# Two key blocks of a sliding-window attention merged into one 128 x 128 square before the transposition

## The chip, the cores and the metric

The kernel runs on one core of one Trainium2 chip. The metric is the time of one execution on the device in microseconds. A core has five engines with a queue of instructions each: TensorE (PE in the profile, with its weight loads apart as PEld), VectorE (DVE), ScalarE (ACT), GpSimd (POOL) and SyncE (SP), which issues most transfers. An engine takes its instructions in the order in which they stand in its queue, and an instruction waits at the head of the queue until the semaphores that it names have come.

## The reference

Attention with a window of 128 keys and 4 sink keys for 4 batches of 8 heads, 768 positions and a head dimension of 64, and then a feed-forward layer with a squared ReLU:

```python
scores = (1 / np.sqrt(D)) * np.matmul(q, k.transpose(0, 1, 3, 2))
is_sink = pos[None, :] < n_sink                  # 4
rel = pos[:, None] - pos[None, :]
keep = is_sink | ((rel >= 0) & (rel < window))   # 128
scores = np.where(keep, scores, -1e9)
a = np.exp(scores - scores.max(-1, keepdims=True))
a = a / (a.sum(-1, keepdims=True) + 1e-9)
x = np.matmul(a, v)                  # then heads side by side: 3072 x 512
h = x @ w_in                         # 512 -> 2048
g = s * np.maximum(h, 0) ** 2 + b
out = g @ w_out                      # 2048 -> 512
```

With a window of 128, a block of 128 queries sees only two blocks of keys besides the sinks: its own (the key's place at or below the query's) and the one before (the key's place above the query's). In a square of 128 x 128 the two parts are disjoint and fill it.

## The kernel before

Everything is fp32 at the ends. The matmuls take numbers split into a high and a low part of a shorter format (tiles `kh` and `kl`, `hl[:, 0]` and `hl[:, 1]`), so that products come as three or two matmuls on the parts.

The 3072 rows are handled in eight chunks of 384 (a half sequence, `half` 0 or 1, of one batch). The feed-forward layer of a chunk (`moe_steps`: 16 groups `l1` of 12 matmuls into `h`, 16 groups `l2` of 9 matmuls into three accumulators `po`) runs while the attention of the next chunk is made; the code calls a step of the one and a slot of the other in turn. The first two chunks' attention comes from `plain_slots`, beside the loading and splitting of the weights; it isn't touched, except for the constants. The other six, four of them second halves, come from `attn_slots`.

There the work is in units (h, i): head h, block i of three blocks of queries. `unit_a` makes the scores `sc` of a unit in PSUM (L297, L298: own block, the block before and 8 sink columns, 264 wide; 136 for the first block of a sequence), then on DVE the masked minimum of the negated scores (L302, with the mask from `msk`; its result is the row's maximum, `negm`), then the exponential on ACT (L308) into `sm`, and a copy of the sink columns on POOL (L310). `unit_b`, two slots later, transposes the two blocks of `sm` (L321, L322) into a PSUM tile `tp`, copies them on ACT into the high part of `hl` (L326) and subtracts on DVE for the low part (L327). `unit_c`, four slots after `unit_a`, multiplies `hl` with the values `vv` into `o` (L360); for i = 1 it takes what became ready for i = 0 and 1, for i = 2 the rest. PSUM tiles `sc`, `tp`, `h`, `o` share five buffers of one pool.

What decides the order in which the instructions stand in each queue is a scheduler. It takes the program in the order of the calls, with the dependences, and by costs of its own it brings forward what can go and puts back what would have to wait. A change in one place can thus move other instructions.

Of the kernel before, what the change touches and what calls it, by code (L numbers as in the profile page):

```python
# [40 lines left out]
def tile_kernel(ctx, tc, qT, kT, k0, v, vsk, n_sink, window, w, s, b, out):  # L41
    nc = tc.nc
    w, n_sink, window = (a.bitcast(I32) for a in (w, n_sink, window))
    const = ctx.enter_context(tc.tile_pool(name="const", bufs=1))
# [87 lines left out]
    def constants2():  # L132

        for i, sel in enumerate(sels):
            spread = wk.tile([P, P], F32, tag="y", name="spread", bufs=1)
            nc.gpsimd.memset(spread, 0.0)
# [5 lines left out]
            nc.scalar.copy(sel, spread)
        for t in psks:
            nc.gpsimd.memset(t, 0.0)
# [6 lines left out]
        mask(m_1[:, 2 * P:], tm2[:, :NS])
        mask(m_even[:, P:P + NS], snk[:, :NS])
        cp = nc.gpsimd.tensor_copy
        upm, lom = m_full[2][:, P:2 * P], m_full[2][:, 2 * P:]
        cp(out=m_0[:, NS:], in_=lom)
        for m, l0 in ((m_1, P), (m_even, P + NS), (m_odd, P)):
            cp(out=m[:, :P], in_=upm)
            cp(out=m[:, l0:l0 + P], in_=lom)
# [126 lines left out]
    def unit_a(k, h, i):  # L285

        hd = k.heads[h]
        pp = k.pairs[h // 2]
# [8 lines left out]
        nc.tensor.matmul(sc[:, :n], hd.qs[:, qs], hd.kh[:, c0:c0 + n], start=True, stop=False)  # L297
        nc.tensor.matmul(sc[:, :n], hd.qs[:, qs], hd.kl[:, c0:c0 + n], start=False, stop=True)  # L298
# [3 lines left out]
        nc.vector.tensor_tensor_reduce(out=sm[:, :n], in0=sc[:, :n], in1=m, scale=-0.125, scalar=BIG,  # L302
                                       op0=ALU.add, op1=ALU.min, accum_out=negm[:, uu])
# [4 lines left out]
        nc.scalar.activation(sm[:, :n], sm[:, :n], AF.Exp, bias=negm[:, uu], scale=-1.0, accum_out=pp.zz[:, i, hh:hh + 1])  # L308
# [1 line left out]
        nc.gpsimd.tensor_copy(out=pp.psk[:, i, :96].rearrange("p (t x) -> p t x", t=3)[:, :, r0:r0 + NS],  # L310
                              in_=sm[:, s0:s0 + NS].unsqueeze(1).to_broadcast([P, 3, NS]))

    def unit_b(k, h, i):

        sm, c0, p0, _ = k.cc.pop((h, i))
# [4 lines left out]
        if p0 is not None:  # L320
            nc.tensor.transpose(tp[:, :P], sm[:, p0:p0 + P], ident)  # L321
        nc.tensor.transpose(tp[:, P:2 * P], sm[:, c0:c0 + P], ident)  # L322

        a, z = (P if p0 is None else 0), 2 * P
        hi, lo = (hd.hl[:, t, i * z + a:(i + 1) * z] for t in range(2))
        nc.scalar.copy(hi, tp[:, a:z])  # L326
        nc.vector.tensor_tensor(out=lo, in0=tp[:, a:z], in1=hi.bitcast(F32), op=ALU.subtract)  # L327
        pp = k.pairs[h // 2]
        if h % 2 == 1 and i == BLK - 1:
            zr = wk.tile([P, 2, BLK, 2], F32, tag="zr", name="zr")  # L330
            zh = wk.tile([P, BLK, 2], F32R, tag="zh", name="zh")
            nc.vector.tensor_scalar(out=zr[:, 0], in0=pp.zz, scalar1=1e-9, scalar2=None, op0=ALU.add)
# [473 lines left out]
```

## Time and profile before

| | us |
|---|---|
| median of 3 executions | 771.59 (771.5 to 771.79) |
| the profiled execution | 772.53 |
| its span, first to last instruction | 770.7 |
| PE, DVE, ACT, POOL busy | 732.8, 492.0, 471.3, 233.3 |

The span has three parts. Up to about 145 us the weights are loaded and split beside the plain attention. From there to 697 us six chunks of attention run beside the MoE of the chunk before; then comes the last chunk's MoE alone. In the profile's rows L12 is line 12 of the kernel, `out<-in` names the tiles, the numbers behind the bar are the group's busy time and the mean ns of one. An entry such as `<-PE sc L298 61.6` says that the engine stood idle for 61.6 us in front of these instructions until that one came. A matmul's duration in a row is longer than the step from one to the next, since matmuls overlap; the chain of waits shows the steps.

### The profile page before, as it was taken

Reading aid. Unit: us, or ns where it says so; the run is one execution under the profiler, and the core shown is the slowest. Engines: PE = TensorE matmul, PEld = TensorE weight load, DVE = VectorE, ACT = ScalarE, POOL = GpSimd, SP = SyncE. Lnnn points to the kernel's source line nnn. Section 1 sums busy time; section 2 is a strip of 40 time slices with the busy share of each in tenths; the row PEclk is TensorE's granted clock in tenths of the full one; section 3 lists DMA queues with packets and bytes.
Section 4 is the critical chain, followed back from the end, with each engine's and each line's share of the span. In section 5 each row is a group of like instructions: output and inputs, shape, how many; then the busy total and the mean of one; then the engine's idle time right before and its main releaser. Section 6 shows DMA issues by size and latency. Waiting matters only on the chain.

```text
span 770.7 us, 11928 instructions
## 1 busy us (share of the span) xinstructions
PE 732.8 (95%) x3988; PEld 649.2 (84%) x3988; DVE 492.0 (64%) x1210; ACT 471.3 (61%) x1176; POOL 233.3 (30%) x380
## 2 busy tenths in 40 slices
PE   7977788899999999999999999999999999999996
PEld 4665577789989899989989899899989999899885
DVE  7879989636676566765676466755676466753321
ACT  4987748537676666646676566656676576643222
POOL 4134633213243332413242242323243233301000
PEclk9999889999999999999999999999999999999999
DMA  8954032022121221112112212112112212001001
GB/s 175 379 216 162 17 125 76 11 80 67 53 53 53 69 56 57 31 50 86 33 44 66 68 46 61 36 51 70 45 45 69 68 43 67 15 1 42 0 1 46
DMA packets 32309, 52.62 MB, mean 68 GB/s; under 512 B 9841, under 2 KB 20721, under 8 KB 30321
## 3 DMA queue, kind: packets, MB, share of 16 engines
q1 hardware_dynamic: 31152, 51.59, 21.8%
q8 instruction: 34, 0.56, 0.3%
q10 hardware_dynamic: 1088, 0.20, 0.2%
q14 instruction: 35, 0.28, 0.1%
HBM read 45.49 MB, written 6.29 MB: 67 GB/s over the span
## 4 chain that ended last, share of the span: by engine, by line
PE 78%; DVE 9%; ACT 3%; issue 2%; POOL 1%; DMA 1%; ACTq 0%; DVEq 0%; POOLq 0%
PE h L575 32%; PE po L593 30%; PE o L360 5%; PE sc L298 2%; PE sc L297 2%; PE tp L322 2%; DVE w L205 2%; PE tp L321 2%; DVE r L579 1%; DVE w L218 1%; DVE wt L204 1%; DVE sm_p L503 1%; DVE g L582 1%; PE o L528 1%; PE os L385 1%
## 5 line engine op out<-in xcount | busy, mean ns | idle before, releaser
L593 PE MATMUL po<-w,g 128*128 128x512 f32 x1152 | 300.1, 403 | 5.1 <-DVE g L582 2.8
L575 PE MATMUL h<-x,w 128*128 128x384 f32 x1536 | 299.8, 344 | 3.3 <-ACT w L212 3.3
L575 PEld LDWEIGHTS h<-x,w 128*128 128x128 f32 x1536 | 268.1, 191 | 10.2 <-ACT w L212 3.7
L593 PEld LDWEIGHTS po<-w,g 128*128 128x128 f32 x1152 | 209.4, 189 | 49.0 <-DVE g L582 5.2
L578 ACT ACTIVATE r<-h 128x384 f32<-128x384 f32 x128 | 62.8, 491 | 121.4 <-PE h L575 117.5
L579 DVE SCALAR_TENSOR_TENSOR r<-r,sb 128x384 f32<-128x384 f32 x128 | 90.0, 703 | 57.9 <-ACT r L578 57.8
L582 DVE SCALAR_TENSOR_TENSOR g<-r,sb,g 128x384 fp32r<-128x384 f32 x128 | 82.6, 645 | 50.0 <-ACT g L581 48.3
L302 DVE CUSTOM_DVE_ANT_0 sm<-sc,msk 128x264 f32<-128x264 f32 (+1 forms) x144 | 59.7, 415 | 79.4 <-PE sc L298 68.6
L581 ACT ACTIVATE g<-r,sb 128x384 fp32r<-128x384 f32 x128 | 78.7, 615 | 32.1 <-DVE r L579 30.2
L310 POOL COPY psk<-sm 128x24 f32<-128x24 f32 x144 | 34.0, 236 | 190.4 <-ACT sm L308 189.5
L308 ACT ACTIVATE sm<-sm,negm 128x264 f32<-128x264 f32 (+1 forms) x144 | 72.8, 505 | 21.0 <-DVE negm L302 19.3
L277 POOL TENSOR_TENSOR kl<-kraw,kh 128x528 fp32r<-128x528 f32 (+1 forms) x48 | 60.0, 1251 | 57.6 <-ACT kh L275 53.5
L326 ACT CAST hl<-tp 128x256 fp32r<-128x256 f32 (+1 forms) x144 | 51.4, 357 | 29.0 <-PE tp L322 28.5
L327 DVE TENSOR_TENSOR hl<-tp,hl 128x256 fp32r<-128x256 f32 (+1 forms) x144 | 58.2, 404 | 10.4 <-ACT hl L326 9.5
L360 PE MATMUL o<-hl,vv 128*128 128x256 f32 (+1 forms) x352 | 61.5, 293 | 0.0
L282 POOL TENSOR_TENSOR vv<-vraw,vv 128x256 fp32r<-128x256 f32 (+1 forms) x48 | 34.5, 719 | 64.2 <-ACT vv L281 61.4
L207 POOL TENSOR_TENSOR w<-w 128x1024 int32<-128x1024 int32 (+1 forms) x17 | 33.0, 1946 | 53.4 <-DVE w L205 24.4
L360 PEld LDWEIGHTS o<-hl,vv 128*128 128x128 f32 x352 | 48.0, 190 | 0.5
L369 DVE TENSOR_TENSOR xm<-o,y 64x384 f32<-64x384 f32 x48 | 26.6, 553 | 30.0 <-ACT y L368 24.4
L298 PE MATMUL sc<-kl,qs 128*128 128x264 f32 (+1 forms) x144 | 41.0, 285 | 0.0
L297 PE MATMUL sc<-kh,qs 128*128 128x264 f32 (+1 forms) x144 | 40.0, 278 | 0.0
L322 PE MATMUL tp<-identr,sm 128*128 128x128 f32 x144 | 39.1, 272 | 0.0
(128 smaller groups left out, 867.3 us busy)
## 6 DMA issues: line engine op xcount, KB each, us to landing
w<-in_w SPq DMA_DIRECT2D x15, 1024.0 KB, 8.1
kraw<-in_kT SPq DMA_DIRECT2D x32, 264.0 KB, 2.6
out<-ot SPq DMA_DIRECT2D x24, 256.0 KB, 2.0
qraw<-in_qT SPq DMA_DIRECT2D x24, 192.0 KB, 2.4
vraw<-in_v SPq DMA_DIRECT2D x16, 256.0 KB, 2.7
kraw<-in_kT SPq DMA_DIRECT2D x16, 200.0 KB, 2.4
vsraw<-in_vsk SPq DMA_DIRECT2D x24, 64.0 KB, 1.8
vraw<-in_v SPq DMA_DIRECT2D x8, 192.0 KB, 2.3
```

What stands on the lines that cost most here:

```text
L277: nc.gpsimd.tensor_tensor(out=hd.kl[:, :kw], in0=hd.k[:, :kw], in1=hd.kh[:, :kw].bitcast(F32), op=ALU.subtract)
L298: nc.tensor.matmul(sc[:, :n], hd.qs[:, qs], hd.kl[:, c0:c0 + n], start=False, stop=True)
L302: nc.vector.tensor_tensor_reduce(out=sm[:, :n], in0=sc[:, :n], in1=m, scale=-0.125, scalar=BIG, op0=ALU.add, op1=ALU.min, accum_out=negm[: ...
L308: nc.scalar.activation(sm[:, :n], sm[:, :n], AF.Exp, bias=negm[:, uu], scale=-1.0, accum_out=pp.zz[:, i, hh:hh + 1])
L327: nc.vector.tensor_tensor(out=lo, in0=tp[:, a:z], in1=hi.bitcast(F32), op=ALU.subtract)
L360: nc.tensor.matmul(hd.o[:, q0:q0 + n * P], hd.vv[:, kb, :], hd.hl[:, t, c0 * P:(c0 + n) * P], start=(hd.n == 0), stop=(i == BLK - 1 and kb ...
L575: nc.tensor.matmul(h[:, :CH], weight[f][:, 0, wi, cc * P:(cc + 1) * P], x[xi][:, cc, :], start=(i == 0), stop=(i == 11))
L578: nc.scalar.activation(r, h[:, :CH], AF.Relu, scale=1.0 / WUP)
L579: nc.vector.scalar_tensor_tensor(out=r, in0=r, scalar=s_ap, in1=r, op0=ALU.mult, op1=ALU.mult)
L581: nc.scalar.activation(gg[:, 0, :], r, AF.Identity, bias=b_ap, scale=1.0)
L582: nc.vector.scalar_tensor_tensor(out=gg[:, 1, :], in0=r, scalar=b_ap, in1=gg[:, 0, :].bitcast(F32), op0=ALU.add, op1=ALU.subtract)
L593: nc.tensor.matmul(po[tb], gg[:, gi, tsl], weight[f][:, 1, wi, :], start=(f == 0 and i == 0), stop=(f == NF - 1 and i == 2))
```

## The change

After the scores, a predicated copy on DVE puts, inside PSUM, the part of the one block that the query can see over the part of the other block that it can't. One square of 128 columns and the 8 sink columns (136) are then masked, reduced and exponentiated in place of 264. Each unit has one transposition, and the three of a head go into one tile `tp`. After the third, the square is taken apart again: what belongs to the block before is copied on ACT (`hi_p`), what belongs to the own block is multiplied by a mask on DVE (`hi_c`), both low parts are subtracted on DVE (`lo_p`, `lo_c`), and three masks on POOL (`affine_select`) put zeros where `hi_p`, `lo_p` and `lo_c` hold the other block's numbers. The matmuls into `o` read `hl` as before.

```diff
-    msk = const.tile([P, 3 * W + P + NS], MDT, tag="msk", name="msk")
+    msk = const.tile([P, 3, P + NS], MDT, tag="msk", name="msk")
+    m_0, m_1, m_2 = (msk[:, j] for j in range(3))
+    is_cur = const.tile([P, P], U8, tag="is_cur", name="is_cur")
+    is_prev = const.tile([P, P], U8, tag="is_prev", name="is_prev")
+    cur_t = const.tile([P, P], MDT, tag="cur_t", name="cur_t")
...
-        for m, l0 in ((m_1, P), (m_even, P + NS), (m_odd, P)):
-            cp(out=m[:, :P], in_=upm)
-            cp(out=m[:, l0:l0 + P], in_=lom)
+        nc.vector.tensor_tensor(out=tmp, in0=low, in1=upp, op=ALU.add)
+        mask(m_2[:, :P], tmp)
+        nc.vector.tensor_scalar(out=is_cur, in0=rel, scalar1=0.0, scalar2=None, op0=ALU.is_ge)
+        nc.vector.tensor_scalar(out=is_prev, in0=rel, scalar1=0.0, scalar2=None, op0=ALU.is_lt)
+        nc.vector.tensor_scalar(out=cur_t, in0=rel, scalar1=0.0, scalar2=None, op0=ALU.is_le)
...
+        a = 0
+        if g % 2:
+            a = P
+            nc.vector.copy_predicated(sc[:, P:2 * P], is_prev, sc[:, :P])
+        elif g:
+            nc.vector.copy_predicated(sc[:, :P], is_cur, sc[:, P + NS:W])
+        n = P + NS
...
-        nc.vector.tensor_tensor_reduce(out=sm[:, :n], in0=sc[:, :n], in1=m, scale=-0.125, scalar=BIG,
-                                       op0=ALU.add, op1=ALU.min, accum_out=negm[:, uu])
+        nc.vector.tensor_tensor_reduce(out=sm[:, :n], in0=sc[:, a:a + n], in1=(m_0, m_1, m_2)[min(g, 2)], scale=-0.125,
+                                       scalar=BIG, op0=ALU.add, op1=ALU.min, accum_out=negm[:, uu])
...
         if i == 0:
+            hd.tp = ps("tp")
+        nc.tensor.transpose(hd.tp[:, i * P:(i + 1) * P], sm[:, c0:c0 + P], ident)
+        if i == BLK - 1:
             hd.hl = wk.tile([P, 2, 2 * CH], F32R, name="hl", tag="hl", bufs=HLB)
-        tp = ps("tp")
-        if p0 is not None:
-            nc.tensor.transpose(tp[:, :P], sm[:, p0:p0 + P], ident)
-        nc.tensor.transpose(tp[:, P:2 * P], sm[:, c0:c0 + P], ident)
...
-        nc.scalar.copy(hi, tp[:, a:z])
-        nc.vector.tensor_tensor(out=lo, in0=tp[:, a:z], in1=hi.bitcast(F32), op=ALU.subtract)
+            i0 = 1 - k.half
+            hi_p, lo_p = (hl[:, t, i0:, 0] for t in range(2))
+            hi_c, lo_c = (hl[:, t, :, 1] for t in range(2))
+            def keep(x, n, cur):
+                d = 1 if cur else -1
+                nc.gpsimd.affine_select(out=x, in_=x, pattern=[[0, n], [d, P]], fill=0.0, base=0, channel_multiplier=-d,
+                                        compare_op=ALU.is_ge if cur else ALU.is_gt)
+            nc.scalar.copy(hi_p, tp[:, i0:])
+            nc.vector.tensor_tensor(out=hi_c, in0=tp, in1=cur_t.unsqueeze(1).to_broadcast([P, BLK, P]), op=ALU.mult)
+            nc.vector.tensor_tensor(out=lo_p, in0=tp[:, i0:], in1=hi_p.bitcast(F32), op=ALU.subtract)
+            nc.vector.tensor_tensor(out=lo_c, in0=tp, in1=hi_c.bitcast(F32), op=ALU.subtract)
+            keep(hi_p, BLK - i0, False)
+            keep(lo_p, BLK - i0, False)
+            keep(lo_c, BLK, True)
```

How the queues change is seen in the order of the built programs. A row names the line, the operation, the tiles and the shape; x9 counts equal rows, and the brackets name whose semaphores the instruction waits for. The lines of the changed kernel are some numbers higher (L332 is the transposition, L386 o, L601 h, L619 po).

TensorE's queue before, for the first head of a second-half chunk, from its second unit's transpositions to its first o:

```order
L321 MATMUL tp<-identr,sm 128x128 [waits DVE_49,Activation_49]
L322 MATMUL tp<-identr,sm 128x128
L593 MATMUL po<-w_522,g 128x512 x9
L297 MATMUL sc<-kh,qs 128x264 [waits DVE_49]
L298 MATMUL sc<-kl,qs 128x264
L321 MATMUL tp<-identr,sm 128x128 [waits DVE_49,Activation_49]
L322 MATMUL tp<-identr,sm 128x128
L360 MATMUL o<-hl,vv 128x256 [waits Activation_49]
L360 MATMUL o<-hl,vv 128x256
L360 MATMUL o<-hl,vv 128x128 x2
```

The same head in the changed kernel, from its third unit's transposition:

```order
L332 MATMUL tp<-identr,sm 128x128 [waits Activation_49]
L619 MATMUL po<-w_524,g 128x512 x2
L619 MATMUL po<-w_524,g 128x512 [waits DVE_49]
L619 MATMUL po<-w_524,g 128x512 x6
L302 MATMUL sc<-kh,qs 128x264 [waits DVE_49,PE_49]
L303 MATMUL sc<-kl,qs 128x264
L332 MATMUL tp<-identr,sm 128x128 [waits PE_49,Activation_49]
L332 MATMUL tp<-identr,sm 128x128 [waits Activation_49]
L619 MATMUL po<-w_583,g 128x512 x3
L386 MATMUL o<-hl,vv 128x256 [waits Pool_49]
```

The first o now stands behind three matmuls of the next group and waits for POOL; three matmuls of an h group follow it, and then the second o, which waits for POOL again.

DVE's queue for the same head, from the predicated copy of its neighbour's scores to the low parts:

```order
L310 COPY_PREDICATED sc<-is_cur,sc 128x128 [waits PE_49]
L605 SCALAR_TENSOR_TENSOR r<-r,sb 128x384 [waits Activation_49]
L314 ISA sm,negm<-sc,msk 128x136 [waits DVE_49,Pool_49]
L314 ISA negm 128x1
L348 TENSOR_TENSOR hl<-tp,cur_t 128x3x128 [waits Activation_49]
L608 SCALAR_TENSOR_TENSOR g<-r,sb,g 128x384 [waits Activation_49]
L349 TENSOR_TENSOR hl<-tp,hl 128x3x128
L350 TENSOR_TENSOR hl<-tp,hl 128x3x128 [waits DVE_49]
```

The product (L348) waits for ACT's copy out of the same PSUM tile, and r and g of the MoE stand between the parts. POOL's queue in a head of a first-half chunk:

```order
L344 AFFINE_SELECT hl<-hl 128x2x128 [waits DVE_49]
L344 AFFINE_SELECT hl<-hl 128x2x128
L282 TENSOR_TENSOR kl<-kraw,kh 128x400 [waits DMAHW3_49,PE_49,Activation_49]
L344 AFFINE_SELECT hl<-hl 128x3x128 [waits DVE_49]
L322 COPY psk<-sm 128x3x8 [waits Activation_49]
```

Here the next head's kl stands between the second and the third mask.

More of the change, by code (lines that the diff above doesn't have):

```diff
@@ L66, in tile_kernel @@
     W = 2 * P + NS
-    msk = const.tile([P, 3 * W + P + NS], MDT, tag="msk", name="msk")
-    m_1, m_odd, m_even = (msk[:, j * W:(j + 1) * W] for j in range(3))
-    m_0 = msk[:, 3 * W:]
+    msk = const.tile([P, 3, P + NS], MDT, tag="msk", name="msk")
[3 more added lines that the diff above has]
+    cur_t = const.tile([P, P], MDT, tag="cur_t", name="cur_t")
     warm = first.tile([P, 512], mybir.dt.bfloat16, tag="warm", name="warm")
@@ L150, in constants2 @@
         mask(m_0[:, :NS], tmp[:, :NS])
[L151 to L155, printed above, removed]
-        for m, l0 in ((m_1, P), (m_even, P + NS), (m_odd, P)):
-            cp(out=m[:, :P], in_=upm)
-            cp(out=m[:, l0:l0 + P], in_=lom)
-        cp(out=m_odd[:, 2 * P:], in_=m_even[:, P:P + NS])
+        mask(m_1[:, P:], tm2[:, :NS])
+        mask(m_2[:, P:], snk[:, :NS])
+        nc.vector.tensor_tensor(out=tmp, in0=low, in1=upp, op=ALU.add)
[3 more added lines that the diff above has]
+        nc.vector.tensor_scalar(out=cur_t, in0=rel, scalar1=0.0, scalar2=None, op0=ALU.is_le)
+        nc.gpsimd.tensor_copy(out=m_0[:, NS:], in_=m_full[2][:, 2 * P:])
+        nc.gpsimd.tensor_copy(out=m_1[:, :P], in_=m_2[:, :P])
     NU = B * H * 2 * BLK
@@ L298, in unit_a @@
         nc.tensor.matmul(sc[:, :n], hd.qs[:, qs], hd.kl[:, c0:c0 + n], start=False, stop=True)
-        m = m_0 if g == 0 else m_1 if g == 1 else m_odd if g % 2 else m_even
+        a = 0
[5 more added lines that the diff above has]
+        n = P + NS
         uu = slice(u, u + 1)
         sm = wk.tile([P, W], F32, name="sm", tag="sm", bufs=SMB)
-        nc.vector.tensor_tensor_reduce(out=sm[:, :n], in0=sc[:, :n], in1=m, scale=-0.125, scalar=BIG,
-                                       op0=ALU.add, op1=ALU.min, accum_out=negm[:, uu])
-        k.cc[(h, i)] = (sm,) + ((NS, None, 0) if g == 0 else (P, 0, 2 * P) if g % 2 else (P + NS, 0, P))
-        s0 = k.cc[(h, i)][3]
+        nc.vector.tensor_tensor_reduce(out=sm[:, :n], in0=sc[:, a:a + n], in1=(m_0, m_1, m_2)[min(g, 2)], scale=-0.125,
+                                       scalar=BIG, op0=ALU.add, op1=ALU.min, accum_out=negm[:, uu])
+        k.cc[(h, i)] = (sm, NS if g == 0 else 0)
+        s0 = 0 if g == 0 else P
         hh = h % 2
@@ L313, in unit_b @@
     def unit_b(k, h, i):
-        sm, c0, p0, _ = k.cc.pop((h, i))
+        sm, c0 = k.cc.pop((h, i))
         hd = k.heads[h]
         if i == 0:
+            hd.tp = ps("tp")
+        nc.tensor.transpose(hd.tp[:, i * P:(i + 1) * P], sm[:, c0:c0 + P], ident)
+        if i == BLK - 1:
             hd.hl = wk.tile([P, 2, 2 * CH], F32R, name="hl", tag="hl", bufs=HLB)
-        tp = ps("tp")
-        if p0 is not None:
[L321 to L327, printed above, removed]
+            tp = hd.tp[:, :CH].rearrange("p (i c) -> p i c", c=P)
+            hl = hd.hl.rearrange("p t (i a c) -> p t i a c", a=2, c=P)
+            i0 = 1 - k.half
[12 more added lines that the diff above has]
+            keep(lo_c, BLK, True)
         pp = k.pairs[h // 2]
```

## The prediction

> **What bounds the kernel now.** I read the page first: the busy table and the chain of work that ended last.
>
> ```profile
> span 770.7 us, 11928 instructions
> PE 732.8 (95%) x3988; PEld 649.2 (84%) x3988; DVE 492.0 (64%) x1210; ACT 471.3 (61%) x1176; POOL 233.3 (30%) x380
> PE 78%; DVE 9%; ACT 3%; issue 2%; POOL 1%; DMA 1%; ACTq 0%; DVEq 0%; POOLq 0%
> ```
>
> TensorE carries 78% of the chain. Next the busy time by stretches, cut where a chunk's first h group starts, for five of the six stretches in which one chunk's MoE runs beside the next one's attention.
>
> ```profile
> core 0: us, PE busy (x) PEld busy (x) DVE busy (x) ACT busy (x) POOL busy (x), PEclk, DMA share, GB/s
> 258.40:347.20 88.80, 88.42 (x512) 81.05 (x511) 56.86 (x146) 57.12 (x150) 29.05 (x53) 1.00 0.19 54
> 347.20:433.10 85.90, 85.39 (x488) 78.04 (x487) 54.57 (x146) 54.87 (x150) 27.63 (x53) 1.00 0.19 55
> ```
>
> PE is busy 88.4 of 88.8 us there, DVE and ACT 57, POOL 29. So TensorE's queue sets the time, and anything that TensorE waits for adds to it in full. What one piece costs is read from the chain in order of time, where pieces follow without a gap:
>
> ```profile
> 447.91 0.12 PE sc L297
> 448.03 0.12 PE sc L298
> 448.16 0.11 PE tp L321
> 448.27 0.11 PE tp L322
> 448.38 0.40 PE o L360 x4
> 448.78 2.17 PE h L575 x12
> ...
> 451.89 2.10 PE po L593 x9
> ```
>
> A pair of score matmuls takes 0.24 us, a transposition 0.11, one h 0.176 (2.11 for twelve in most groups), one po 0.234, one 256-wide o 0.10.
>
> **Term 1, what goes.** The groups by line and shape give the count of the transpositions of the previous block:
>
> ```profile
> L321 PE MATMUL tp<-identr,sm 128*128 128x128 f32 x128 | 35.0, 274 | 0.0
> L302 DVE CUSTOM_DVE_ANT_0 sm<-sc,msk 128x264 f32<-128x264 f32 x128 | 55.0, 430 | 72.2 <-PE sc L298 61.6 <-PE tp L322 9.8
> L302 DVE CUSTOM_DVE_ANT_0 sm<-sc,msk 128x136 f32<-128x136 f32 x16 | 4.7, 294 | 7.2 <-PE sc L298 7.0
> L302 DVE DVE_READ_ACCUMULATOR2_ANT negm<- 128x1 f32 x144 | 11.8, 82 | 0.0
> L327 DVE TENSOR_TENSOR hl<-tp,hl 128x256 fp32r<-128x256 f32 x128 | 53.7, 419 | 9.9 <-ACT hl L326 9.1
> L327 DVE TENSOR_TENSOR hl<-tp,hl 128x128 fp32r<-128x128 f32 x16 | 4.6, 286 | 0.5 <-ACT hl L326 0.3
> L388 DVE TENSOR_TENSOR xm<-os,xm 128x384 f32<-128x384 f32 x24 | 12.8, 553 | 6.1 <-PE os L385 5.8
> ```
>
> All 128 go. Their 274 ns are pipelined; on the chain each is worth 0.11 us: 128 x 0.11 = **-14.1 us**, all on the path.
>
> **What it adds elsewhere, off the path by its sum.** Per unit with two blocks DVE gains a predicated copy of 128 columns in PSUM. No row shows one; the nearest read PSUM at that width (0.286 and 0.294), so I take 0.29, with 0.20 below (POOL's 128-wide memset, further down, as the cheapest 128-wide pass) and 0.42 above (the 256-wide row, if it read both operands in turn). The masked minimum falls from 0.430 to 0.294, with its 0.08 read-out as before. Per head of a second-half chunk three subtractions of 0.419 become three passes over 384 columns (0.553, by L388: one operand in PSUM). DVE: 3 x (0.29 + 0.294) + 3 x 0.553 - 3 x (0.430 + 0.419) = +0.86 us per head, some 7 per stretch: 57 becomes 64 of 88. ACT loses work (264-wide exponentials become 136 wide, three copies one): worth nothing, since it was covered by PE. POOL gains three masks per head.
>
> **Term 2, the wait that takes the place.** Before, the first o of a head needed a copy on ACT (0.37) and a subtraction on DVE (0.42) of an earlier unit, and both lay under the next slot. Now all of a head's transposed weights come out together after its third transposition, through ACT copy, DVE product, DVE subtraction, and three masks in turn on POOL; the second o (the low half) needs the last mask. The order now puts o behind a fixed amount of other PE work. I set t = 0 at the end of the third transposition and compare arrival with readiness. The masks' price, a for 384 columns and b for 256, is bounded by POOL's rows:
>
> ```profile
> masks.py:199 POOL TENSOR_SCALAR_AFFINE_SELECT idraw<-idraw 128x128 f32<-128x128 f32 x1 | 0.3, 292 | 0.0
> L158 POOL COPY msk<-m_all 128x128 bf16<-128x128 bf16 x3 | 0.9, 295 | 0.0
> L310 POOL COPY psk<-sm x144: 193/203/529, 174.1 to 681.8; 128x24 f32<-128x24 f32 x144
> L136 POOL MEMSET spread<- 128x128 f32 x2 | 0.4, 198 | 0.0
> L144 POOL MEMSET psk<- 128x384 f32 x2 | 0.8, 415 | 0.1
> L282 POOL TENSOR_TENSOR vv<-vraw,vv 128x256 fp32r<-128x256 f32 x32 | 24.0, 750 | 37.6 <-ACT vv L281 35.2 <-POOL psk L310 0.7
> L391 POOL TENSOR_TENSOR x<-xm,x 128x384 fp32r<-128x384 f32 x24 | 24.1, 1014 | 30.2 <-ACT x L390 29.9
> L277 POOL TENSOR_TENSOR kl<-kraw,kh 128x400 fp32r<-128x400 f32 x16 | 17.0, 1061 | 15.1 <-ACT kh L275 15.1
> ```
>
> The mask instruction itself is there at 128 columns: 0.292, as a POOL copy of that width (0.295). Copies of 24 and 128 columns differ by 0.092 over 104 columns, 0.88 ns each; memsets of 128 and 384 by 0.85. So a = 0.292 + 256 x 0.88 = **0.52**, b = 0.40. Below: 0.29, if width cost nothing. Above: the slope of POOL's two-operand rows, (1014 - 750) / 128 = 2.1 ns a column, put on the 0.292, gives 0.83. I take 0.52, because copy and mask agree at 128.
>
> Hand-overs cost 0.03 to 0.04 us: ACT's copy at 448.61 ends at 448.98 and DVE starts at 449.01.
>
> ```profile
> 448.61 0.37 ACT L326 CAST hl<-tp 128x256 fp32r<-128x256 f32 x1
> 448.78 1.34 POOL L277 TENSOR_TENSOR kl<-kraw,kh 128x528 fp32r<-128x528 f32 x1 [1.69 <-ACT kh L275]
> 449.01 0.43 DVE L327 TENSOR_TENSOR hl<-tp,hl 128x256 fp32r<-128x256 f32 x1 [0.26 <-ACT hl L326]
> 449.51 0.63 DVE L332 TENSOR_SCALAR zr<-zz 128x6 f32<-128x6 f32 x1
> ...
> 457.32 0.61 DVE L579 SCALAR_TENSOR_TENSOR r<-r,sb 128x384 f32<-128x384 f32 x1
> 457.97 0.55 DVE L276 TENSOR_TENSOR qs<-qraw,qs 64x384 fp32r<-64x384 f32 x1
> 458.13 0.46 POOL L310 COPY psk<-sm 128x24 f32<-128x24 f32 x1 [2.39 <-ACT sm L308]
> 458.62 0.62 DVE L582 SCALAR_TENSOR_TENSOR g<-r,sb,g 128x384 fp32r<-128x384 f32 x1
> ```
>
> The commonest head is the one whose new order is shown with the change. DVE has the predicated copy of the score issued just before (ends 0.22), the MoE square r (0.61, to 0.83), the masked minimum (0.37, to 1.20), the product hi_c (0.55, to 1.75; ACT's copy, which it waits for, ends by 0.7), g (0.62, to 2.38), the subtraction lo_p (0.55, to 2.93). POOL starts at 2.97 and the third mask ends at 2.97 + 3a = 4.53. PE meanwhile has nine po (2.10), a score pair (0.24), two transpositions (0.22), three po (0.70): the first o is due at 3.27 and needs 2.97 + a = 3.49, a wait of 0.22; with one o and three h more the second is due at 3.90 unwaited. So PE loses 4.53 - 3.90 = 0.63 in all. Behind it on PE's queue stand the next h and everything else; nothing passes it.
>
> The other places in a second-half chunk (there are four such chunks, 32 heads), by the same sums: one head with DVE's xm ahead in the queue, ready 4.16, due 3.50: 0.66; one with no r and g, ready 3.29, due 3.03: 0.26; one ready 4.53, due 4.20: 0.33; the last one, with DVE free, ready 3.25, due 2.91: 0.34; one is due at 5.85 and waits for nothing. Three of the common kind: 3 x 0.63. A chunk loses 3.5 us. In the two first-half chunks lo_p is 0.13 shorter and two masks are b wide, but in three heads the order puts the next head's kl (1.06) between POOL's second and third mask: 2.84 + 2 x 0.40 + 1.06 + 0.52 = 5.22 against 3.84, 3.84 and 4.02: 1.38, 1.38 and 1.20. Three more wait 0.57, 0.14 and 0.12, two not at all. A chunk loses 4.8 us. Sum: 4 x 3.5 + 2 x 4.8 = **+23.5 us**. A predicated copy at its ends of 0.20 or 0.42 moves most of these chains by -0.09 or +0.13, the sum by some -3 or +4.
>
> **Term 3, POOL and DVE in each other's way.** In the last fence POOL's copy of 24 columns, 0.203 as a rule, took 0.46 while DVE ran L276, and ended just after it; DVE's L332 took 0.63 and ended with POOL's kl. L327, with one operand in PSUM, kept its 0.43 beside the same kl. Now L276, or r, follows the last subtraction on DVE in most heads, just when POOL's third mask is due. That can hold the mask by up to 0.55 in each of the 40 heads that wait, 22 us; I take a bit over a third, **+8**, with 0 to 22 as its ends.
>
> The Trainium skill has this as a rule (SBUF — State Buffer, Who interferes with whom): a VectorE instruction with two SBUF inputs, or in a 2-port mode, and a GpSimd one that reads SBUF exclude each other for a whole instruction, whoever issues first. The rows agree in both directions. By the rule taken strictly the term would be near its upper end and the sum 14 us higher.
>
> **Term 4, start.** Three 128-wide masks, an add and a mask more on DVE, which is on the chain before 145 us; five POOL copies fewer. About **+1** (0 to 3).
>
> **Sum.** 770.7 - 14.1 + 23.5 + 8 + 1 = 789.1 us of span. The profiled execution took 772.53, 1.8 more than its span, and lies 0.9 above the median 771.59; so the median becomes 789.1 + 0.9 = **790 us**.
>
> **Rivals.**
> *The masks are hidden (faster).* If a 384-wide mask costs what the 128-wide one does, 0.29, the common head is ready at 3.84, before 3.90, and all second-half chunks wait for nothing; only kl keeps 2.7 us per first-half chunk. 770.7 - 14.1 + 5.4 + 1 + 0.9 = 764; 758 if kl's place hurts nothing either. For it: the transpositions surely leave the path, and a 32- and a 128-partition mask cost alike. Against: memset and copy grow with width. It decides below a of about 0.43, where waits equal the 14.1 saved if Term 3 is nothing.
> *POOL is as slow as with two operands (much slower).* a = 0.83, b = 0.56: 10.0 and 8.6 us per chunk, 57 in all, so 824. For it: r and g collide too. Against: the 0.292 row.
> *Waits eat the gain exactly*, 771.6: nothing draws it there.
> *It does not do what it says*: excluded, the new order holds one transposition per unit.
> *DVE becomes the bound*: 64 of 88 us; it would need 24 more per stretch. Not given a chance.
>
> **How the numbers follow.** Forecast 0.65, slow POOL 0.12, hidden masks 0.17, no change 0.06. About 0.2% is what this kernel's measurement can tell from none. Slower 0.77, same 0.06, faster 0.17. The forecast's own range, from a = 0.45 with nothing for Term 3 to a = 0.6 with all of it, is 775 to 813; reaching into both sides it is 762 to 818.
>
> **What would show it.** Right: PE waits of 0.2 to 1.4 us in front of o, released by POOL's masks, in about 40 heads; stretches of 90 to 93 us instead of 88.8 and 85.9; masks near 0.52. Wrong: PE without gaps and stretches of 86 (then the masks were cheap or early), a predicated copy near 0.6 us, or waits in front of transpositions instead of o.

## The result and the profile after

The changed kernel takes **807.38 us** (median of 4 runs, 805.91 to 809.24), the kernel before 771.69 beside it: a ratio of 1.0459 (95% interval 1.0438 to 1.0480), slower. The forecast was 790 with a range of 762 to 818: the direction and the range were right, the time is 17 us above the forecast. The profiled execution took 809.24 us with a span of 807.5.

The page of the changed kernel, engine sums and the chain by engine:

```profile
span 807.5 us, 11922 instructions
PE 745.0 (92%) x3860; PEld 638.5 (79%) x3860; DVE 542.3 (67%) x1343; ACT 437.7 (54%) x1080; POOL 312.2 (39%) x518
PE 59%; DVE 19%; ACT 8%; POOL 7%; issue 4%; DMA 2%; SPq 1%; POOLq 0%; ACTq 0%; DVEq 0%
```

TensorE's share of the chain fell from 78% to 59%, although it has 128 matmuls less to do; POOL, which carried 1%, carries 7%, and DVE 19% instead of 9%. The stretches from one chunk's first h group to the next (columns as in the prediction: length, busy time of each engine, granted clock):

```profile
265.17:360.25 95.08, 90.87 (x488) 79.11 (x487) 66.29 (x170) 51.23 (x134) 43.46 (x77) 0.98 0.18 51
360.25:452.51 92.26, 86.90 (x471) 75.84 (x470) 62.18 (x162) 49.34 (x134) 39.49 (x77) 1.00 0.17 51
452.51:546.07 93.56, 89.38 (x487) 77.88 (x486) 66.25 (x170) 51.19 (x134) 43.46 (x77) 1.00 0.18 51
```

They were 88.80 and 85.90. The time before the first such stretch grew by 0.54 us (170.28 against 169.74) and the last piece, without attention, is 74.4 as before. So all of it is in these six stretches: 526.7 us before, 562.8 now. The groups behind that, by shape:

```profile
L344 POOL TENSOR_SCALAR_AFFINE_SELECT hl<-hl 128x384 fp32r<-128x384 f32 x112 | 64.6, 605 | 19.9 <-DVE hl L349 19.9
L344 POOL TENSOR_SCALAR_AFFINE_SELECT hl<-hl 128x256 fp32r<-128x256 f32 x32 | 12.4, 406 | 10.1 <-DVE hl L349 9.7
L308 DVE COPY_PREDICATED sc<-is_prev,sc 128x128 f32<-128x128 uint8 x80 | 23.2, 290 | 46.0 <-PE sc L303 44.6
L350 DVE TENSOR_TENSOR hl<-tp,hl 128x384 fp32r<-128x384 f32 x48 | 26.2, 546 | 0.0
L386 PEld LDWEIGHTS o<-hl,vv 128*128 128x128 f32 x352 | 51.7, 192 | 53.1 <-POOL hl L344 52.5
```

The last row carries the verdict: the weight loads in front of o stood idle for 53.1 us, 52.5 of them ended by POOL's masks, in 80 places. The predicted prices hold: 0.29 for the predicated copy, 0.55 for a DVE pass over a head, 0.41 for a 256-wide mask.

### The profile page after: what moved, and what is told of

Same layout as the page of the kernel before. It is cut to its first block, busy times and chain, and to the rows that moved or that the text cites. A ratio compares the mean times of both kernels' runs of the same rounds, so it can differ in the third digit from the quotient of the medians.

```text
span 807.5 us, 11922 instructions
## 1 busy us (share of the span) xinstructions
PE 745.0 (92%) x3860; PEld 638.5 (79%) x3860; DVE 542.3 (67%) x1343; ACT 437.7 (54%) x1080; POOL 312.2 (39%) x518
## 4 chain that ended last, share of the span: by engine, by line
PE 59%; DVE 19%; ACT 8%; POOL 7%; issue 4%; DMA 2%; SPq 1%; POOLq 0%; ACTq 0%; DVEq 0%
PE h L601 26%; PE po L619 21%; POOL hl L344 6%; PE o L386 5%; DVE g L608 3%; DVE r L605 2%; ACT r L604 2%; DVE w L210 2%; DVE hl L348 2%; DVE hl L349 1%; PE sc L303 1%; PE sc L302 1%; DVE sm L314 1%; DVE wt L209 1%; DMA q<-in_qT 1%
## 5 line engine op out<-in xcount | busy, mean ns | idle before, releaser
L619 PE MATMUL po<-w,g 128*128 128x512 f32 x1152 | 313.3, 408 | 7.4 <-ACT g L607 3.9
L601 PE MATMUL h<-x,w 128*128 128x384 f32 x1536 | 303.1, 344 | 0.0
L601 PEld LDWEIGHTS h<-x,w 128*128 128x128 f32 x1536 | 269.2, 191 | 6.0 <-POOL x L417 1.9
L619 PEld LDWEIGHTS po<-w,g 128*128 128x128 f32 x1152 | 209.6, 191 | 46.5 <-ACT g L607 4.8
L608 DVE SCALAR_TENSOR_TENSOR g<-r,sb,g 128x384 fp32r<-128x384 f32 x128 | 100.5, 786 | 42.0 <-ACT g L607 41.2
L320 ACT ACTIVATE sm<-sm,negm 128x136 f32<-128x136 f32 x144 | 57.9, 402 | 92.4 <-DVE negm L314 92.0
L322 POOL COPY psk<-sm 128x24 f32<-128x24 f32 x144 | 41.7, 290 | 158.7 <-ACT sm L320 158.3
L386 PE MATMUL o<-hl,vv 128*128 128x256 f32 (+1 forms) x352 | 73.5, 308 | 24.9 <-POOL hl L344 22.7
L386 PEld LDWEIGHTS o<-hl,vv 128*128 128x128 f32 x352 | 51.7, 192 | 53.1 <-POOL hl L344 52.5
L344 POOL TENSOR_SCALAR_AFFINE_SELECT hl<-hl 128x384 fp32r<-128x384 f32 (+1 forms) x144 | 76.6, 560 | 30.0 <-DVE hl L349 29.6
L282 POOL TENSOR_TENSOR kl<-kraw,kh 128x528 fp32r<-128x528 f32 (+1 forms) x48 | 64.6, 1345 | 13.4 <-ACT kh L280 8.2
L287 POOL TENSOR_TENSOR vv<-vraw,vv 128x256 fp32r<-128x256 f32 (+1 forms) x48 | 33.9, 707 | 68.9 <-ACT vv L286 66.9
L308 DVE COPY_PREDICATED sc<-is_prev,sc 128x128 f32<-128x128 uint8 x80 | 23.2, 290 | 46.0 <-PE sc L303 44.6
L314 DVE CUSTOM_DVE_ANT_0 sm<-sc,msk 128x136 f32<-128x136 f32 x144 | 42.3, 294 | 13.6 <-PE sc L303 8.4
L281 DVE TENSOR_TENSOR qs<-qraw,qs 64x384 fp32r<-64x384 f32 x48 | 38.3, 798 | 2.8 <-ACT qs L277 0.6
```

Of the source, the lines that this page charges most:

```text
L282: nc.gpsimd.tensor_tensor(out=hd.kl[:, :kw], in0=hd.k[:, :kw], in1=hd.kh[:, :kw].bitcast(F32), op=ALU.subtract)
L314: nc.vector.tensor_tensor_reduce(out=sm[:, :n], in0=sc[:, a:a + n], in1=(m_0, m_1, m_2)[min(g, 2)], scale=-0.125, scalar=BIG, op0=ALU.add, ...
L344: nc.gpsimd.affine_select(out=x, in_=x, pattern=[[0, n], [d, P]], fill=0.0, base=0, channel_multiplier=-d, compare_op=ALU.is_ge if cur els ...
L386: nc.tensor.matmul(hd.o[:, q0:q0 + n * P], hd.vv[:, kb, :], hd.hl[:, t, c0 * P:(c0 + n) * P], start=(hd.n == 0), stop=(i == BLK - 1 and kb ...
L601: nc.tensor.matmul(h[:, :CH], weight[f][:, 0, wi, cc * P:(cc + 1) * P], x[xi][:, cc, :], start=(i == 0), stop=(i == 11))
L608: nc.vector.scalar_tensor_tensor(out=gg[:, 1, :], in0=r, scalar=b_ap, in1=gg[:, 0, :].bitcast(F32), op0=ALU.add, op1=ALU.subtract)
```

## One head, and where the sum was short

This is the commonest head of the prediction, in a second-half chunk (order of time: start, length, engine, line, what; in brackets the idle time before and what ended it). Its third transposition starts at 277.42:

```profile
277.42 0.27 PE L332 MATMUL tp<-identr,sm 128*128 128x128 f32 x1
...
280.43 1.78 POOL L344 TENSOR_SCALAR_AFFINE_SELECT hl<-hl 128x384 fp32r<-128x384 f32 x3 [0.48 <-DVE hl L349]
281.00 0.19 PEld L386 LDWEIGHTS o<-hl,vv 128*128 128x128 f32 x1 [0.49 <-POOL hl L344]
281.00 0.38 PE L386 MATMUL o<-hl,vv 128*128 128x256 f32 x1
281.14 0.69 DVE L281 TENSOR_TENSOR qs<-qraw,qs 64x384 fp32r<-64x384 f32 x1
281.23 0.68 PE L601 MATMUL h<-x,w 128*128 128x384 f32 x3
...
282.27 0.56 PE L386 MATMUL o<-hl,vv 128*128 128x256 f32 x3 [0.36 <-POOL hl L344]
```

The prediction had t = 0 at 277.42 + 0.11 = 277.53, the first o ready at 3.49 and the second at 4.53. Measured: 281.00 is 3.47, and 282.27 is 4.74. Two things are not in the sum. First, the weights of a stopped o are loaded after the stop: load and matmul start together at 281.00, and h follows 0.23 us later, where an o that did not wait took 0.10 (the row of 448.38 in the prediction). Each stop so costs some **0.11 us more** than the lateness of its mask. Second, three masks took 1.78 us instead of 1.47 (0.52 for one, 0.475 from one's start to the next's): the third is longer. Taken apart, in another head:

```profile
299.99 0.52 POOL L344 TENSOR_SCALAR_AFFINE_SELECT hl<-hl 128x384 fp32r<-128x384 f32 x1 [0.27 <-DVE hl L349]
...
300.80 0.62 DVE L605 SCALAR_TENSOR_TENSOR r<-r,sb 128x384 f32<-128x384 f32 x1
...
300.94 0.86 POOL L344 TENSOR_SCALAR_AFFINE_SELECT hl<-hl 128x384 fp32r<-128x384 f32 x1
```

The third mask ends 0.38 after DVE's r (0.34 longer than alone). In the head above it was qs (281.14 to 281.83) in place of r. Counted in the trace, the third mask took 0.84 us or more in 29 of the 48 heads, and 0.52 in the others.

The sixth head of a second-half chunk fell out of the sum altogether: predicted 0.33, measured 0.94 + 0.87 in PE's own waits.

```profile
512.06 1.34 POOL L282 TENSOR_TENSOR kl<-kraw,kh 128x528 fp32r<-128x528 f32 x1 [0.53 <-ACT kh L280]
512.18 1.63 DVE L281 TENSOR_TENSOR qs<-qraw,qs 64x384 fp32r<-64x384 f32 x1
...
513.99 0.27 PE L332 MATMUL tp<-identr,sm 128*128 128x128 f32 x1
514.07 0.53 DVE L358 TENSOR_SCALAR zr<-zz 128x6 f32<-128x6 f32 x1
...
516.99 0.55 DVE L348 TENSOR_TENSOR hl<-tp,cur_t 128x384 fp32r<-128x384 f32 x1
...
518.69 1.78 POOL L344 TENSOR_SCALAR_AFFINE_SELECT hl<-hl 128x384 fp32r<-128x384 f32 x3 [0.48 <-DVE hl L349]
519.26 0.39 PE L386 MATMUL o<-hl,vv 128*128 128x256 f32 x1 [0.94 <-POOL hl L344]
...
520.52 0.56 PE L386 MATMUL o<-hl,vv 128*128 128x256 f32 x3 [0.87 <-POOL hl L344]
```

Here kl holds DVE: qs took 1.63 us instead of 0.55, so at the transposition's end (514.10) zr, g and xm still stood ahead of this head's own work in DVE's queue, and the masks began 4.6 us after it, where the common head has 2.97. In e11 below, which leaves kl out, the masks of this head begin 3.49 us after the transposition: so 1.1 of the 1.6 us are kl's, and the rest is what stands in DVE's queue anyway.

The theory to test: (W) TensorE stops in front of o for POOL's masks, by their chain, by holds between POOL and DVE, and by the open weight load. Its rivals: (B) gathering three units makes the halves late, whoever masks; (D) the added work on DVE and POOL slows everything.

## Experiments

**e1: no masks.**

```diff
-            keep(hi_p, BLK - i0, False)
-            keep(lo_p, BLK - i0, False)
-            keep(lo_c, BLK, True)
```

> This kernel leaves out the three masking passes on POOL per head (so both halves of the square go unmasked into the output matmuls); all else is the changed kernel. Theory W (TensorE stops in front of o for the masks): the changed kernel's five whole stretches are 4.7 to 6.4 us longer than before although 24 and 16 transpositions of 0.11 us are gone, so some 50 us of waits are in it; without masks they vanish: 807.4 - 50 = 757 us (753 to 763), stretches of about 86.2 and 84.1 us (88.8 - 24 x 0.11, 85.9 - 16 x 0.11), and next to no idle time of the weight load in front of o. Rival B (gathering three units before splitting makes the halves late, whoever masks): o still waits, now for DVE's subtractions, and the time stays above 780. Rival D (DVE's and POOL's added work slows everything through the MoE's r and g): above 795, since DVE keeps all its work.

Measured: 765.5 us (one run). The waits for POOL are gone, but the time is 8 us above the forecast and just outside its range. The waits in front of o (who waited for whom: us in total, times, longest):

```profile
PEld o L383 <- DVE hl L350: 7.5, 15, 0.7
PEld o L383 <- DVE hl L348: 1.5, 4, 0.4
```

o now waits 9 us for DVE's passes themselves. The six stretches sum to 522.4 us. So W holds for some 40 of the 50 us, and a small B is there under it: the last subtraction (L350), which by the prediction's figures for the common head ends at 2.93 + 0.55 = 3.48, before the second o is due at 3.90, comes too late in 15 places.

**e2: a fourth mask.**

```diff
             keep(lo_c, BLK, True)
+            keep(lo_c, BLK, True)
```

> Adds a fourth masking pass per head (the low half of the own block once more, which changes no value). Theory W: the passes follow each other every 0.475 us on POOL, and in some 42 of 48 heads the second o waits for the last of them: + 42 x 0.475 = +20 us, 827 (821 to 836, the upper end if a VectorE instruction with two SBUF inputs holds the fourth pass too). Rivals B and D: POOL is off the path, below +5 us, 807 to 812.

Measured: 827.92 us (one run), +20.5 us; the wait of PEld rose by 21.4:

```profile
PEld o L387 <- POOL hl L344: 73.9, 80, 1.8
```

What POOL adds there, TensorE pays in full. B and D are out as the main cause.

**e3: r with one operand in PSUM.**

```diff
-nc.scalar.activation(r, h[:, :CH], AF.Relu, scale=1.0 / WUP)
-nc.vector.scalar_tensor_tensor(out=r, in0=r, scalar=s_ap, in1=r, ...)
+nc.scalar.activation(r, h[:, :CH], AF.Relu, scale=1.0 / WUP ** 2)
+nc.vector.scalar_tensor_tensor(out=r, in0=h[:, :CH], scalar=s_ap, in1=r, ...)
```

> The MoE's square r on DVE reads h from PSUM as one of its two operands (h x s x relu(h)/65536 instead of s x relu(h/256) squared, the same value), so that it has one SBUF input; nothing else differs. Lock theory: in the changed kernel the third mask took 0.84 to 0.88 us in some 33 of 48 heads instead of 0.52, ending 0.38 us after r's end; with r no longer excluding POOL these masks fall to 0.52, and some 26 heads whose second o waits win 0.33 us each: 807.4 - 8 = 799 us (796 to 802). Rival (the third mask is long for another reason, its own shape or the semaphore of the last subtraction): it stays at 0.84 and the time within 2 us of 807.

Measured: 795.0 us, 1.0292 of before (1.0256 to 1.0328), 12.4 less than the changed kernel.

```profile
L605 DVE SCALAR_TENSOR_TENSOR r<-h,sb,r 128x384 f32<-128x384 f32 x128 | 78.8, 616 | 64.5 <-ACT r L604 62.8
L344 POOL TENSOR_SCALAR_AFFINE_SELECT hl<-hl 128x384 fp32r<-128x384 f32 x112 | 60.0, 563 | 19.7 <-DVE hl L349 19.7
```

r fell from 705 to 616 ns, and 14 long masks are left of 29 (not of 33, as the expectation said). The hold by r is shown, but not as the only one. In the profiled execution, one of the faster ones (793.36 us), the six stretches are 9.2 us shorter than in the changed kernel; some 4 of these belong to the granted clock, which is 1.00 in all six here and 0.98 in three of the changed kernel's (last section). The chunk-0 stretch, which has no masks, is 5.8 shorter, and that was not foreseen (e6).

**e4: the output matmuls two units later.**

```diff
-LB, LC, LD, L2 = 2, 4, 1, 2
+LB, LC, LD, L2 = 2, 6, 1, 2
```

> One number: a head's output matmuls are issued two units later (six units behind the scores instead of four), so that by the order 7 to 9 us of other TensorE work stand between the third transposition and o instead of 2.4 to 4.2. Theory W: the masks are ready 3.3 to 5.2 us after the transposition, so no o waits, and the gain of the transpositions is left: 771.6 - 14 + up to 2 for the end of each chunk = 758 us (754 to 764). Rival D: the time stays above 795, because DVE and POOL do the same work. A new wait could take the place: the value tiles (two buffers) come free two units later, and the next heads' split on ACT and POOL with them; if that bites, o or the scores wait for vv or kl, some 0.5 us a head, 780.

Measured: 771.82 us, 0.9977 of before (0.9961 to 0.9994): 35 us won against the changed kernel, but not the 758 expected. No o waits any more, as W had it. A new wait took the place, at another spot than the one I named:

```profile
PE os L411 <- DVE xsk L402: 9.2, 6, 1.9
```

One of the six in order of time:

```profile
483.76 1.64 POOL L282 TENSOR_TENSOR kl<-kraw,kh 128x528 fp32r<-128x528 f32 x1
...
484.23 1.20 DVE L358 TENSOR_SCALAR zr<-zz 128x6 f32<-128x6 f32 x1
...
486.74 0.55 DVE L402 TENSOR_TENSOR xsk<-ts,xsk 32x384 fp32r<-32x384 f32 x1
...
487.35 0.44 PE L411 MATMUL os<-xsk,vs 128*128 128x384 f32 x1 [1.87 <-DVE xsk L402]
```

zr, six columns wide, took 1.20 us beside kl; xsk queued behind it, and os stopped for xsk (it waited 2.3 us in all in the changed kernel). The clock has a share too: three of e4's four second-half stretches have 0.98 and take 89.5 to 89.9 us, the fourth has 1.00 and takes 88.5.

**e5: split per unit.** Each unit's square is split and masked right after its own transposition:

```diff
-            hd.tp = ps("tp")
-        nc.tensor.transpose(hd.tp[:, i * P:(i + 1) * P], sm[:, c0:c0 + P], ident)
-        if i == BLK - 1:
...
-            keep(hi_p, BLK - i0, False)
+        tp = ps("tp")[:, :P]
+        nc.tensor.transpose(tp, sm[:, c0:c0 + P], ident)
...
+        hi_c, lo_c = (hl[:, t, i, 1] for t in range(2))
...
+            keep(hi_p, False)
+            keep(lo_p, False)
+        keep(lo_c, True)
```

> The changed kernel, but each unit's square is split by itself right after its transposition (its own PSUM tile, copies, product, subtractions and three masks over 128 columns), not three units together; scores, counts of transpositions and output matmuls stay. Chain theory (o is late because three masks of a whole head stand in a row behind the head's last transposition): the last unit's chain is only some 0.29 x 3 on DVE and 0.26 x 3 on POOL, so its low half is ready about 2.9 us after the transposition with r and the minimum in between, before the 3.0 to 3.9 us at which o is due; most waits vanish, though POOL's masks cost more in sum (9 x 0.27 = 2.4 us a head instead of 1.5) and DVE's passes too (9 x 0.29 = 2.6 instead of 1.65): 771.7 - 14 + 6 = 764 us (756 to 774). Rival (POOL's total mask time is what PE pays): above 807. Rival (DVE, at 66 of 93 us, has no room for 8 us more per stretch): 790 or more.

Measured: **758.65 us**, 0.9811 of before (0.9794 to 0.9827). A second-half and a first-half stretch:

```profile
254.32:340.53 86.21, 85.65 (x488) 78.53 (x487) 66.77 (x218) 52.42 (x150) 51.88 (x125) 1.00 0.19 56
340.53:424.80 84.27, 83.56 (x471) 76.26 (x470) 63.38 (x202) 50.21 (x142) 46.02 (x109) 1.00 0.19 56
```

The masks there, by shape:

```profile
L340 POOL TENSOR_SCALAR_AFFINE_SELECT hl<-hl 128x128 fp32r<-128x128 f32 x400 | 145.7, 387 | 52.9 <-ACT g L607 36.8
```

The masks cost twice as much in sum (145.7 us against 77.0) and DVE and POOL are busier than in the changed kernel, and no o waits for them. So it is neither the amount of POOL's work nor DVE's that made the change slow, but three long masks in a row at the end of a head's chain. The stretches also give the first term its measure: 88.80 - 86.21 = 2.59 for 24 transpositions, 85.87 - 84.27 = 1.60 for 16, so 0.10 to 0.11 us each; over the six stretches -13.5 (in e9 below -14.9).

**e6: the kernel before with e3's r.**

The edit is e3's.

> The kernel before, with only the MoE's r read from PSUM as in e3. In e3 the stretch from chunk 0's first h to chunk 1's fell from 128.0 to 122.2 us, where no attention of the new kind runs, so 6 of its 12 us had nothing to do with the masks. If so, the kernel before gains them too: 771.7 - 6 = 766 us (763 to 769), all in that stretch, the others within 0.3 us since TensorE is busy 99% of them. Otherwise, if the gain of e3 was the masks' alone, 771.7 within 1.

Measured: 765.76 us, 0.9909 (0.9893 to 0.9926), all of it in the chunk-0 stretch, the others being 88.55, 88.81 and 85.87. That stretch in e6:

```profile
41.50:162.04 120.54, 102.35 (x490) 82.70 (x488) 98.47 (x173) 84.42 (x166) 52.44 (x38) 0.97 0.28 98
```

and in the kernel before:

```profile
42.31:169.74 127.43, 106.78 (x489) 86.30 (x488) 103.60 (x173) 83.66 (x166) 51.92 (x38) 0.93 0.27 93
```

DVE has 5.1 us less to do there, and the granted clock is higher, 0.97 against 0.93. How much is r's and how much the clock's stays open: in e7 and e9, with the same r, that stretch took 125.7 at a clock of 0.92.

**e7 and e8: e4 with r, and with r and g, from PSUM.** e7 is e4 and e3 together; e8 has, beyond it:

```diff
-nc.vector.scalar_tensor_tensor(out=r, in0=h[:, :CH], scalar=s_ap, in1=r, ...)
-nc.scalar.activation(gg[:, 0, :], r, AF.Identity, bias=b_ap, scale=1.0)
-nc.vector.scalar_tensor_tensor(out=gg[:, 1, :], in0=r, scalar=b_ap, ...)
+nc.vector.scalar_tensor_tensor(out=h[:, :CH], in0=h[:, :CH], scalar=s_ap, in1=r, ...)
+nc.scalar.activation(gg[:, 0, :], h[:, :CH], AF.Identity, bias=b_ap, scale=1.0)
+nc.vector.scalar_tensor_tensor(out=gg[:, 1, :], in0=h[:, :CH], scalar=b_ap, ...)
```

> The output matmuls two units later (as in e4) and r from PSUM (as in e3). In e4 no o waited for a mask any more, but the stretch of chunk 0 kept its 127.4 us and the second-half stretches took 88.5 to 89.9, with os waiting up to 2.1 us for a DVE queue in which a 6-column zr took 1.20 us beside POOL's kl. Expected by adding up: 771.8 - 6 for the first stretch - 4 x 1 for the second-half ones = 762 us (757 to 767). If the two gains overlap or os keeps its wait: 766 to 770.

> As e7, and DVE writes r back over h in PSUM, so that g's subtraction, too, has one operand in PSUM and one in SBUF (g took 0.786 us on average in the changed kernel, 0.55 is what a pass of 384 columns with one PSUM operand takes). Lock theory: DVE gets 0.2 x 16 = 3 us a stretch back, POOL's kl and masks are held less: 757 us (752 to 763). Rival: the PSUM bank of h is held until g is done, some 1.3 us longer, and with five banks in turn TensorE waits for one: 765 to 780, with waits in front of h, sc or tp.

Measured: e7 766.9 us (0.9921, 0.9904 to 0.9937), what was expected if os keeps its wait, and it does. e8 762.22 (0.9858, 0.9842 to 0.9875), with no wait for the bank of h; 5 us above its forecast, since the wait for xsk stays here too.

**e9 and e10: e5 with r, and with r and g, from PSUM.** The edits of e3 and e8 on e5.

> Split per unit (as in e5) and r from PSUM (as in e6). In e5 the stretches stand at 86.2 and 84.3 us, what the kernel before has less its removed transpositions, so there is no wait left for r to shorten; only the stretch of chunk 0 can gain, which went from 127.4 to 120.5 us in e6. Adding up: 758.7 - 5 = 753.5 us (751 to 757). If the two share a limit there: 757 to 759.

> As e9, with r written over h in PSUM and g read from there (as in e8). TensorE sets the stretches, DVE has room, so g's shorter hold brings nothing there: within 2 us of e9, 753 (750 to 757). If the longer use of h's bank bites, now that each unit has a transposition bank of its own: 760 or more, with waits in front of h, sc or tp.

Measured: **e9 754.36 us, 0.9755 of before (0.9731 to 0.9779)**, the fastest of all. e10 759.63 (0.9829, 0.9808 to 0.9850): the rival happened, 5 us above e9. Its first-half stretches are 86.35 instead of 84.26, and in one of them TensorE's loads wait for the bank that g holds:

```profile
PEld h L601 <- DVE g L608: 1.9, 3, 0.8
```

e8 had no such wait; e10 takes three banks a head for its transpositions, e8 one.

**e11 and e12: no kl, and no kl with r and g from PSUM.**

```diff
-hd.kl = wk.tile([P, KW], F32R, tag="kl", name="kl")
...
-nc.gpsimd.tensor_tensor(out=hd.kl[:, :kw], in0=hd.k[:, :kw], in1=hd.kh[:, :kw].bitcast(F32), op=ALU.subtract)
...
-nc.tensor.matmul(sc[:, :n], hd.qs[:, qs], hd.kl[:, c0:c0 + n], ...)
+nc.tensor.matmul(sc[:, :n], hd.qs[:, qs], hd.kh[:, c0:c0 + n], ...)
```

> The changed kernel without POOL's kl: the low half of the keys is neither computed nor used, the second score matmul reads the high half again (so the scores are wrong; TensorE's work and its order around the masks stay, 2.4 to 4.2 us of other matmuls between the last transposition and o). It tells how much of the waits comes from kl, which stands between POOL's second and third mask in three heads of a first-half chunk, and beside which DVE's qs took 1.63, its zr 0.53 and its g 1.38 us instead of 0.55, 0.06 and 0.62. kl theory: of some 50 us of waits the heads with kl in between (6 x about 1) and the sixth head of a second-half chunk, which came 1.6 us later than the sum said (4 x 1.9), go: 807.4 - 14 = 793 us (787 to 798). Chain theory, as the prediction's sum had it (only the three heads gain): 807.4 - 5 = 802 (800 to 805).

> e11, and r and g with one operand in PSUM (as in e8): now next to no pair of VectorE and POOL instructions with SBUF inputs on both sides is left around the masks. What is left should be the bare chain of the prediction's second term without kl (3.5 us per second-half chunk, about 2.3 per first-half chunk: 18.6) and the weight load that each stopped o has in the open (0.11 us x about 80 = 8.8): 771.7 - 14.1 + 27 = 785, less 3 for the stretch of chunk 0: 782 us (778 to 786). If holds are not what makes the rest: within 3 us of e11.

Measured: e11 789.84 us (1.0231, 1.0211 to 1.0250), e12 783.07 (1.0146, 1.0123 to 1.0169), both within 4 us of the kl and the hold theory. The waits of the loads in front of o in e11:

```profile
PEld o L384 <- POOL hl L342: 41.1, 74, 1.0
```

and in e12:

```profile
PEld o L384 <- POOL hl L342: 34.1, 70, 0.7
```

Some holds are left in e12, since qs still has two SBUF operands: the third mask takes 0.84 us in 16 heads, against 26 in e11. The expectation of e11 gives zr alone as 0.06 us; in the traces it takes 0.17, and where it took 0.53 (the head above), POOL ran vv and no longer kl.

The time of the six stretches and what it loses against e5, whose o does not wait (513.2 us):

| kernel | six stretches, us | lost |
|---|---|---|
| before | 526.7 | 13.5 (the transpositions) |
| changed | 562.8 | 49.6 |
| e11, no kl | 547.1 | 33.9 |
| e12, no kl, r and g from PSUM | 540.7 | 27.5 |
| e3, r from PSUM | 553.6 | 40.4 |
| e1, no masks | 522.4 | 9.2 |
| e2, a fourth mask | 583.1 | 69.9 |
| e4, o two units later | 526.9 | 13.7 |

## Why the prediction was right in its direction and short in its size

**Term 1, -14.1: right.** -13.5 in e5 and -14.9 in e9, 0.10 to 0.12 us a transposition.

**What lies off the path: right.** DVE 66 and 62 us a stretch (64 forecast), the predicated copy 0.290, the passes 0.55.

**Term 2, +23.5: the mechanism right, two costs missing.** 42 of 48 heads wait in front of o, single waits of 0.2 to 1.5 us; the mask alone is 0.52 and 0.41. For the common head the first o was forecast at 3.49 and came at 3.47. What failed is the step that counts only a mask's lateness: the load of a stopped o stands behind the stop, 0.11 us by the rows of the head above, and 0.11 x 80 stops = 8.8 us if every stop costs as much. The step that failed in the sixth head is the time at which DVE gets to the head's own work: the masks began 1.6 us later than in the common head, and this chunk's wait of 0.33 there became 1.8. The second missing cost is the clock, some 4 us (last section).

**Term 3, +8: the mechanism right, mis-sized.** From the table: without kl 15.7 less, with r and g from PSUM another 6.4. Of the 15.7, Term 2 already held 6.4: by its own figures the three heads with kl between the masks would wait 0.32, 0.32 and 0.14 without kl's 1.06, and a first-half chunk 1.6 instead of 4.8 (the expectations of e11 and e12 put 5 and 2.3 there). Some 4 more belong to the clock, which is 1.00 in all of e11's stretches. That leaves 15.7 - 6.4 - 4 + 6.4 = 11.7 us in place of 8. The direction that I had not summed is the one shown in the sixth head: POOL's kl holding DVE's qs, so that the masks start late; the prediction put the hold on the mask alone.

The Trainium skill (SBUF — State Buffer, Who interferes with whom) says that a VectorE instruction with two SBUF inputs or in a 2-port mode and a GpSimd one that reads SBUF exclude each other, and that one with a single SBUF input, outside the 2-port modes, does not contend. The trace agrees on both: r went from 705 to 616 ns on average with an operand in PSUM, and DVE's last subtraction (L350), with one operand in PSUM, kept its 0.55 though it runs beside the first mask. By the rule taken strictly I had 22 for this term; that was too much, since a mask is held only where such an instruction happens to stand beside it.

**The whole sum.** The kernel loses 49.6 us, and the forecast had 31.5. Since Term 3 was got above by subtraction, only the chain without kl and the load, 4 x 3.5 + 2 x 1.6 + 8.8 = 26.0, can be held against a measurement, e12's 27.5. That they lie so close is in part luck: 16 masks of e12 are still held by some 0.32 us each, some 5 us, so its bare chain comes out shorter than the 17.2 of the sum. A count that needs no such split takes each TensorE matmul's start to the next one's, less the median of that step in the kernel before, and compares with e5. By it the changed kernel loses 34.2 us in front of o, 9.7 behind an o (the load) and 5.7 elsewhere, 4.1 of these at half clock. So the waits that Terms 2 and 3 forecast at 31.5 came to 34.2, and most of what was short are the two costs that the sum put at nothing. Of the signs named, the waits in about 40 heads and the masks near 0.52 came true; the stretches, 92.2 to 95.1 us, lie mostly above the 90 to 93 for the same reason.

**Term 4, +1: right**, 0.5.

**Rivals.** "The masks are hidden" falls by e2, "POOL is as slow as with two operands" by the 0.52. That a delay of o would hide them (e4) and that shorter chains would (e5) was not among the rivals, as the change did neither.

## What to carry to other kernels

Where work is gathered to save issue overhead, count the length of the chain behind the last piece, not the sum: cut into short pieces the masks took twice the time in sum (e5), and the kernel was 49 us faster. For every instruction on such a chain look at what can stand ahead of it in its engine's queue, and at VectorE and GpSimd instructions beside it that both read SBUF; one operand in PSUM took the hold away for r (e3), but keeping h's bank longer for g cost time in e10. A wait in front of a matmul cost the open weight load too here, 0.11 us a stop.

## What was not expected

**The granted clock falls after the stops.** In the sixth head of a second-half chunk TensorE stops twice within 3.4 us. The clock's own record has three windows of 3.41 us at half clock in the six stretches of the changed kernel, at 239.01, 334.58 and 706.63, each right behind such a pair of stops. The gaps between them are whole numbers of 3.41 us (28 and 109), so they lie on one grid. On this grid, the second of these places, and the fourth such head, which kept its clock:

```profile
331.17:334.58 3.41, 1.82 (x9) 1.45 (x10) 3.35 (x8) 1.84 (x6) 3.27 (x5) 1.00 0.01 2
334.58:337.99 3.41, 3.41 (x13) 2.94 (x12) 0.84 (x4) 0.00 (x0) 0.32 (x1) 0.50 0.22 60
515.49:518.90 3.41, 2.84 (x17) 2.54 (x15) 3.41 (x10) 2.42 (x8) 0.67 (x3) 1.00 0.12 43
518.90:522.31 3.41, 2.17 (x10) 1.75 (x11) 3.25 (x7) 1.49 (x5) 3.38 (x5) 1.00 0.02 5
522.31:525.73 3.42, 3.42 (x22) 3.25 (x22) 0.72 (x4) 1.27 (x4) 0.77 (x2) 1.00 0.23 60
```

Where both stops fall into one window of the grid, TensorE is busy for 1.82 of 3.41 us (1.61 and 1.60 in the other two places) and the next window runs at 0.50. In the fourth head the grid cuts the stops in two, the window has 2.17 us of work, and the clock stays at 1.00. The stops themselves are the same (0.94 and 0.87 us); the phase of the grid makes the difference. The three stretches with such a window take 94.8 to 95.1 us, the one without 93.56: some 4 us in all. The kernel before has 1.00 in every such stretch, and so has e11, without the long double stop.

The Trainium skill (TensorE: Matmul & The Clock Gate, What's actually happening) tells of a clock halved after a window of about 3.4 us without work, and of windows that run freely. The trace agrees on the half, on the length and on the free run; but here no window was without work, TensorE was busy for 47 to 53% of it. Nor is the busy share alone the condition: over the grids of all these traces after the first 40 us, the clock fell behind windows up to 57% busy, and some of 44 to 57% were passed over. What decides between them these runs do not tell.

**A six-column instruction of 1.20 us.** zr (L358, 128 x 6) mostly takes 0.17 us; it took 0.81 beside kl in the head of 277.42, and 1.20 in e4, where os then stopped for 1.87 us. The length of an instruction says little here about how long it holds its queue.
